# Hedgehog attention gated by a SwiGLU block: the last stage's transposes move from TensorE to VectorE, and its small products take two token tiles in one run

## The chip, the core and the metric

The kernel runs on one core of a Trainium2 chip. The metric is the device time of one execution in microseconds. The core has a matmul engine (TensorE, "PE" in the profile, with its weight loads listed apart as "PEld"), VectorE ("DVE"), ScalarE ("ACT"), GpSimd ("POOL") and a queue that starts transfers (SyncE, "SP"). Each engine works its own instructions in order and waits for others on semaphores.

## The reference

With x of 2048 tokens by 1024 channels, everything in float32:

```python
xn = layernorm(x)
q, k, v = split(xn @ wqkv)                      # 32 heads of 32 channels
pq, pk = per head: q @ w_phi, k @ w_phi
phi_q = concat(softmax(pq), softmax(-pq))       # 64 features per head
phi_k = concat(softmax(pk), softmax(-pk))
kv = phi_k^T v ;  z = sum over tokens of phi_k
o  = (phi_q kv) / (phi_q z + 1e-6)              # per head
s  = o @ wo
g  = silu((silu(xn @ w1) * (xn @ w3)) @ w2)
out = x + s * g
```

## The kernel before

Tokens come in 16 tiles of 128. Large float32 products are made of three passes of a high and a low part (`split` makes them: ScalarE casts the high part, VectorE subtracts it), and by Strassen's scheme with seven products for eight. The stages, in order of time:

1. Layer norm, the operands, and `xn @ w1`, `xn @ w3` (up to about 1160 us).
2. Passes one and two: keys and values, `kv` and `z`.
3. Pass three (`queries`, about 1493 to 1646 us): eight pairs of tiles. `spikes` turns 16 heads of one tile (128x512) into exponentials `e` (128x1024: for each head 32 exponentials of p - max and 32 of min - p) and stores them to DRAM (`e_d`). It is called four times for a pair. A list `later` holds VectorE's less urgent work; one item of it is issued per product. The two tiles of `EARLY` are weighted here already (their sums, factors and scaling run through `later`).
4. The product with `w2`: seven blocks `kb` of eight steps, one pair of tiles each, to about 2170 us. In the last block ScalarE forms the gate (`gate`), which goes to DRAM (`g_d`), and the buffers that come free take what the last stage needs.
5. The last stage (from about 2170 us), whose order is written out by hand for all engines, one tile per turn of the loop:
   - `load_e` brings `e` of a tile back. `weigh` (GpSimd) multiplies it with z; `add_up` (VectorE) sums `e` and the weighted `ez` over each 32 values; `factors` makes the factors out of the sums; `scale` multiplies `e` by them (one half on VectorE, one on GpSimd).
   - `turned`: 16 TensorE transposes of 128x128, and four ScalarE copies out of PSUM (`et`).
   - `heads_out`: 32 small products (64 rows by 32 columns, 128 tokens) with `kvu` into `po`, and `split` of `po` into the operands `oT`.
   - `half_out`: 24 matmuls of 128x512 with `wos` into `pm`, twice a tile, once for each half of the output columns.
   - `result`: VectorE multiplies `pm` by the gate, GpSimd adds x, a transfer stores the half row.

TensorE's order in a turn is: 16 transposes of the next tile, 24 matmuls, 32 small products of the next tile, 24 matmuls. A float32 product that isn't split takes two records of the trace, so the 32 small products show as 64.

Of the kernel before, what the change touches and what calls it, by code (L numbers as in the profile page):

```python
# [21 lines left out]
G = 8  # L22
# [6 lines left out]
def tile_kernel(ctx: ExitStack, tc: tile.TileContext, x, wkT, wqT, wv, wphi, wo, w1, w3, w2, out):  # L29
# [49 lines left out]
    e_d = [[dram.tile([P, D], F, name=f"e_d{i}_{c}") for c in range(2)] for i in range(NT)]  # L79
# [3 lines left out]
    kvu_d = dram.tile([P, 2 * G, DH], F, name="kvu_d")  # L83
# [632 lines left out]
    early, later = {}, []  # L716

    def spikes(t, c, p, e, scaling=False):

        mm = small.tile([P, 2, 16], F, name="mm2")  # L720
        p3 = p.rearrange("p (h f) -> p h f", f=DH)
        nc.vector.tensor_reduce(mm[:, 0, :], p3, axis=AX.X, op=OP.max)
        nc.vector.tensor_reduce(mm[:, 1, :], p3, axis=AX.X, op=OP.min)
        e4 = e.rearrange("p (h s f) -> p h s f", s=2, f=DH)
        nc.vector.tensor_sub(e4[:, :, 0], p3, mm[:, 0, :].unsqueeze(2).to_broadcast([P, 16, DH]))
        nc.vector.tensor_sub(e4[:, :, 1], mm[:, 1, :].unsqueeze(2).to_broadcast([P, 16, DH]), p3)
        nc.scalar.activation(e, e, AF.Exp)
        if not scaling:
            nc.scalar.dma_start(e_d[t][c], e)
            return  # L730

        ef = e.rearrange("p (h f) -> p h f", f=DH)
# [3 lines left out]
        sm, by, rho = early["s"][0][:, c], early["s"][1][:, c], small.tile([P, 2, 16], F, name="rho")  # L736
# [17 lines left out]
        def scale():  # L754
            nc.vector.tensor_mul(ef, ef, by.rearrange("p h s -> p (h s)").unsqueeze(2).to_broadcast([P, H, DH]))
            nc.sync.dma_start(e_d[t][c], e)

        later.extend((sum_e, sum_ez, factors, scale))

    EARLY = (3, 5)  # L760
# [5 lines left out]
    def queries(i, xo, wb, steps, pend):  # L766

        t0, t1 = pairs[i]
        if i == EARLY[0] - 1:
            early["z"] = [flat(bpa.tile([P, 2, 512], R, name="ze", tag=f"ra{6 + c}").bitcast(F)) for c in range(2)]  # L770
            load_z(early["z"])
        for an, pb in seven(xo, wb):
# [3 lines left out]
            elif an == "A12":  # L776
# [4 lines left out]
                spikes(t0, 0, k0, early["e"][0] if i in EARLY else e01[:, 0], i in EARLY)  # L781
# [3 lines left out]
            elif an == "S1":  # L785
                if pend:
                    kv(*pend)
                    kv_out(1, pkv)
                d1 = work.tile([P, 512], F, name="d1", tag="w")
                nc.scalar.copy(d1, pb)  # L790
            elif an == "S3":
                nc.vector.tensor_add(d1, pb, d1)
                spikes(t1, 1, d1, e01[:, 1])
            elif an == "S4":
                nc.vector.tensor_add(d0, pb, d0)
                e10 = rwp.tile([P, 2, 1024], F, name="eq", tag="rw")
                spikes(t0, 1, d0, early["e"][1] if i in EARLY else e10[:, 0], i in EARLY)
            else:
                spikes(t1, 0, pb, e10[:, 1])
# [88 lines left out]
    for c in range(3):  # L888
# [5 lines left out]
        for i in range(len(pairs)):  # L894
# [33 lines left out]
            assert not (end and later)  # L928
            xo = nxt
        wb = wbn  # L930
    close("big")
# [6 lines left out]
    def acc_of(i):  # L938
        for j, t in enumerate(pairs[i]):
            if t not in acc:  # L940
                tag = f"acc{t}" if i < 4 else "acc" + "EEEZZZWW"[2 * i - 8 + j]
                acc[t] = accp.tile([P, 2, 512], F, name=f"acc{t}", tag=tag, bufs={"E": 3, "Z": 3, "W": 2}.get(tag[3], 1))
# [4 lines left out]
    wos, es, ez, sums, by = {}, {}, {}, {}, {}  # L947
# [10 lines left out]

    TILES = [pairs[i][0] for i in EARLY]
    TILES += [t for t in range(NT) if t not in TILES]  # L960
    E_TAGS = (("0", "4"), ("2", "6"), ("1", "5"), ("7", "W"))

    def load_e(i):

        es[i] = []
        for c in range(2):
            tag = E_TAGS[i % 4][c]
            es[i].append(accp.tile([P, 1024], F, name="e", tag=f"acc{tag}", bufs=2 if tag == "W" else 1))
            nc.sync.dma_start(es[i][c], e_d[TILES[i]][c])

    def weigh(i, c):

        t = accp.tile([P, 1024], F, name="ez", tag="accE", bufs=3)
        nc.gpsimd.tensor_mul(t, es[i][c], zb[c])  # L974
        ez[i, c] = t

    def add_up(i, c):

        if c == 0:
            sums[i] = small.tile([P, 2, 2, 16, 2], F, name="sums")  # L980
        for m, src in enumerate((es[i][c], ez.pop((i, c)))):
            nc.vector.tensor_reduce(sums[i][:, m, c].rearrange("p h s -> p (h s)"), src.rearrange("p (h f) -> p h f", f=DH),
                                    axis=AX.X, op=OP.add)

    def factors(i, eng, rho, den):

        sm = sums.pop(i)
        by[i] = small.tile([P, 2, 16, 2], F, name="by")
        nc.vector.reciprocal(rho, sm[:, 0, :, :, 1])
        eng.tensor_mul(rho, sm[:, 0, :, :, 0], rho)  # L990
        eng.tensor_mul(den, sm[:, 1, :, :, 1], rho)
        eng.tensor_add(den, sm[:, 1, :, :, 0], den)
        nc.vector.reciprocal(by[i][:, :, :, 0], den)
        eng.tensor_mul(by[i][:, :, :, 1], by[i][:, :, :, 0], rho)

    def scale(i, c, eng, f=None):

        f = by[i][:, c] if f is None else f
        e3 = es[i][c].rearrange("p (h f) -> p h f", f=DH)
        eng.tensor_mul(e3, e3, f.rearrange("p h s -> p (h s)").unsqueeze(2).to_broadcast([P, H, DH]))  # L1000
# [31 lines left out]
    for r, new in enumerate(steps):  # L1032
# [10 lines left out]
        for b, an, bn in TURN:  # L1043
# [3 lines left out]
            elif old:  # L1047
                product(*old, banks, r, second, b, an, bn)
                if new is None and bn == "T1":
                    load_wo(14)  # L1050
                    load_wo(15)
        if new:
            second = a_second(*parts) if r else ready[1]
        if 8 <= r < 24:
            c, j, s = (r - 8) // 8, (r - 8) // 2 % 4, r % 2
            q = 64 * (j % 2) + 32 * s
            nc.sync.dma_start(kvu_d[q:q + 32, G * c + j // 2:G * c + G:2], kv_d[c][32 * j:32 * j + 32, 4 * s:4 * s + 4])
# [4 lines left out]
        if i + 1 == len(pairs):  # L1062
            if end:
                for k in range(8, 14):
# [6 lines left out]
        if end:  # L1071
            if i:
                gate(*pairs[i - 1])
            if i in (1, 2):
                for k in range(4 * i - 4, 4 * i):
                    load_wo(k)
# [3 lines left out]
            elif i == 2:  # L1080
                load_e(0)
            elif i == 4:
                load_e(1)
                load_e(2)
            elif i == 5:
                kvu = accp.tile([P, 2 * G, DH], F, name="kvu", tag="acc3")
                nc.sync.dma_start(kvu, kvu_d)
        old, banks = new, bank
    close("ps")
# [4 lines left out]
    gate(*pairs[-1])  # L1094
    in_order(ENG.PE, ENG.SP, ENG.Activation, ENG.DVE, ENG.Pool)
    load_e(3)
    weigh(2, 0)
    weigh(2, 1)
    stat = ps.tile([P, 2, 256], F, name="stat", bufs=1)
    po = ps.tile([P, 2, 2, 2, P], F, name="po", bufs=1)  # L1100

    def turned(e):

        ets = []
        for m in range(4):
            pt = ps.tile([P, 4, P], F, name="pt2", tag="tr", bufs=3)
            for g in range(4):
                nc.tensor.transpose(pt[:, g, :], e[m // 2][:, (4 * (m % 2) + g) * P:(4 * (m % 2) + g + 1) * P], ident)
            ets.append(work.tile([P, 4, P], F, name="et", tag="w"))
            nc.scalar.copy(ets[m], pt)  # L1110
        return ets

    def heads_out(ets):

        oT = []
        for c in range(2):
            for q in range(2):
                for g in range(4):
                    for hh in range(2):
                        sl = slice(64 * hh, 64 * hh + 64)  # L1120
                        nc.tensor.matmul(po[32 * g:32 * g + 32, hh, c, q], kvu[sl, G * c + 4 * q + g], ets[2 * c + q][sl, g],
                                         start=True, stop=True, skip_group_check=True)
        for c in range(2):
            oT.append(quad("oT"))
            o4 = oT[c].rearrange("p u (h q) t -> p u h q t", q=2)
            split(o4[:, 0], o4[:, 1], po[:, :, c])
        return oT

    def half_out(oT, c):

        p = ps.tile([P, 512], F, name="pm", tag="mm", bufs=2)
        n = 0
        for k in range(8):
            for a, b in PASSES:
                nc.tensor.matmul(p, oT[k // 4][:, a, k % 4], wos[c, k][:, b], start=n == 0, stop=n == 23)  # L1135
# [3 lines left out]
    def load_gx(i, c):  # L1139

        gx[i, c] = accp.tile([P, 2, 512], F, name="gx", tag="accZ", bufs=3)
        t = TILES[i]
        nc.sync.dma_start(gx[i, c][:, 0], g_d[t][:, c * 512:c * 512 + 512])
        nc.sync.dma_start(gx[i, c][:, 1], x[t * P:(t + 1) * P, c * 512:c * 512 + 512])

    def result(i, c, p):

        t = gx.pop((i, c))
        nc.vector.tensor_mul(t[:, 0], p, t[:, 0])
        (nc.vector if i + 1 == NT else nc.gpsimd).tensor_add(t[:, 0], t[:, 0], t[:, 1])  # L1150
        r0 = TILES[i] * P
        nc.sync.dma_start(out[r0:r0 + P, c * 512:c * 512 + 512], t[:, 0])

    gx = {}
    load_gx(0, 0)
    load_gx(0, 1)
    oT = heads_out(turned(es.pop(0)))
    p1 = None
    for i in range(NT):
        nxt = i + 1 < NT  # L1160
        st = stat[:, i % 2]
        rho, den, by0 = (st[:, a:a + 32].rearrange("p (c h) -> p c h", c=2) for a in (0, 32, 64))
# [68 lines left out]
```

## Time and profile before

| | |
|---|---|
| median of three runs | 2406.64 us (2405.56 to 2408.09) |
| profiled execution | 2406.6 us, its span 2404.8 us |
| TensorE busy, share of the span | 2367.7 us, 98% |
| VectorE, ScalarE, GpSimd busy | 73%, 37%, 30% |
| last stage, from the end of the product with w2 | about 2170 to 2404.8 us |
| 768 large matmuls of the last stage | 183.0 us busy |
| 256 transposes, 1024 records of small products | 34.2 us and 18.7 us busy |

Busy times are sums over the instructions of one group; a group's row gives also the mean duration of one. Matmuls overlap their neighbours, so the time from the start of one run of matmuls to the start of the next is read for what a run costs, not the sum of durations. The profiled execution took 1.8 us more than its span.

### The profile page before, as it was taken

What the parts mean: (1) busy time and instruction counts of PE and PEld (TensorE: products, weight loads), DVE (VectorE), ACT (ScalarE), POOL (GpSimd) and SP (SyncE); (2) the same over time, 40 slices, a digit from 0 to 9 for tenths busy, and PEclk for the clock granted to TensorE, in tenths of its full rate; (3) what the DMA queues carried; (4) which work ended last, traced back from release to release, by engine and by line L of the source; (5) the groups of instructions that cost most, each with busy time, mean ns of one, the idle gap of its engine ahead of it and who ended that gap; (6) DMA issues with size and microseconds to landing.
All of it is one profiled execution on the core that took longest, in us unless ns stands there. A gap on an engine that the chain in (4) does not pass through costs nothing.

```text
span 2404.8 us, 36324 instructions
## 1 busy us (share of the span) xinstructions
PE 2367.7 (98%) x13554; PEld 1950.3 (81%) x13554; DVE 1746.5 (73%) x2493; ACT 891.8 (37%) x1566; POOL 726.4 (30%) x511
## 2 busy tenths in 40 slices
PE   5999999999999999999999999999999999999999
PEld 5888888888888888888888788887888888887887
DVE  8567798775688888884676556786677887776664
ACT  6445544443345445443221112334322322243221
POOL 2233555452355555551000000010011111124663
PEclk9999999999999999999999999999999999999999
DMA  7567789877877787877999868987544354466553
GB/s 262 177 213 238 231 293 311 286 248 230 255 274 267 248 284 263 278 250 258 361 329 357 303 190 322 363 330 252 165 156 130 143 182 175 171 242 236 188 177 114
DMA packets 305679, 586.33 MB, mean 244 GB/s; under 512 B 25440, under 2 KB 140384, under 8 KB 302816
## 3 DMA queue, kind: packets, MB, share of 16 engines
q1 hardware_dynamic: 301472, 569.34, 68.4%
q10 hardware_dynamic: 4032, 14.68, 1.5%
q8 instruction: 107, 1.75, 0.3%
q14 instruction: 68, 0.56, 0.1%
HBM read 379.19 MB, written 205.00 MB: 243 GB/s over the span
## 4 chain that ended last, share of the span: by engine, by line
PE 90%; issue 4%; POOL 3%; DVE 1%; DMA 1%; ACT 1%; SPq 0%; POOLq 0%; ACTq 0%; DVEq 0%
PE bankb L622 25%; PE bankb L1013 13%; PE bankc L622 13%; PE bankb L673 11%; PE bankc L1013 6%; PE banka L622 6%; PE bankc L673 5%; PE banka L1013 3%; PE banka L673 3%; PE pm L1135 2%; POOL ez L974 1%; POOL e L1000 1%; PE pkv L659 1%; POOL gx L1150 1%; PE pw L246 1%
## 5 line engine op out<-in xcount | busy, mean ns | idle before, releaser
L92 DVE TENSOR_TENSOR bo<-rw,bo 128x512 fp32r<-128x512 f32 x336 | 310.1, 923 | 147.4 <-ACT bo L91 145.0
L1023 POOL TENSOR_TENSOR acc<-acc,u 128x512 f32<-128x512 f32 x48 | 63.7, 1327 | 476.6 <-ACT u L1022 447.0
L91 ACT CAST bo<-rw 128x512 fp32r<-128x512 f32 x336 | 201.3, 618 | 7.9 <-DMA w_d0T<-w2o 3.2
L1013 PE MATMUL bankb<-bo,as 128*128 128x512 f32 x816 | 200.8, 389 | 0.0
L1135 PE MATMUL pm<-wos,oT 128*128 128x512 f32 x768 | 183.0, 394 | 0.0
L1013 PEld LDWEIGHTS bankb<-bo,as 128*128 128x128 f32 x816 | 153.1, 188 | 32.2 <-ACT acc L1019 0.4
L1135 PEld LDWEIGHTS pm<-wos,oT 128*128 128x128 f32 x768 | 141.9, 188 | 31.8 <-issue 2.8
L622 PE MATMUL bankc<-op0S,bo 128*128 128x512 f32 x672 | 163.1, 391 | 1.4 <-ACT op0S L91 1.4
L622 PE MATMUL bankb<-op0A,bo 128*128 128x512 f32 x672 | 163.3, 391 | 0.3 <-DVE bo L92 0.3
L622 PE MATMUL bankb<-op0S,bo 128*128 128x512 f32 x672 | 162.9, 391 | 0.0
L622 PE MATMUL bankc<-op1S,bo 128*128 128x512 f32 x672 | 161.5, 389 | 0.4 <-issue 0.4
L622 PE MATMUL bankb<-op1S,bo 128*128 128x512 f32 x672 | 161.5, 389 | 0.0
L622 PE MATMUL bankb<-op1A,bo 128*128 128x512 f32 x672 | 161.4, 389 | 0.0
L622 PEld LDWEIGHTS bankc<-op0S,bo 128*128 128x128 f32 x672 | 125.4, 188 | 27.7 <-ACT op0S L91 1.6
L622 PEld LDWEIGHTS bankc<-op1S,bo 128*128 128x128 f32 x672 | 126.0, 188 | 26.9 <-issue 0.7
L1013 PE MATMUL bankc<-bo,as 128*128 128x512 f32 x576 | 146.5, 389 | 1.1 <-ACT as L91 0.7
L622 PEld LDWEIGHTS bankb<-op1S,bo 128*128 128x128 f32 x672 | 126.0, 188 | 26.5 <-ACT wk L564 0.4
L622 PEld LDWEIGHTS bankb<-op1A,bo 128*128 128x128 f32 x672 | 126.1, 188 | 26.2
L622 PEld LDWEIGHTS bankb<-op0A,bo 128*128 128x128 f32 x672 | 125.4, 188 | 26.3 <-DVE bo L92 0.6
L622 PEld LDWEIGHTS bankb<-op0S,bo 128*128 128x128 f32 x672 | 125.4, 188 | 26.2 <-ACT wk L564 0.2
L127 POOL TENSOR_TENSOR rw<-rw 128x512 f32<-128x512 f32 x56 | 86.3, 1541 | 155.0 <-DMA rw<-in_w 137.1
L1013 PEld LDWEIGHTS bankc<-bo,as 128*128 128x128 f32 x576 | 108.0, 188 | 24.3 <-ACT as L91 1.1
(246 smaller groups left out, 4730.2 us busy)
## 6 DMA issues: line engine op xcount, KB each, us to landing
rw<-in_w SPq DMA_DIRECT2D x224, 256.0 KB, 3.5
hr<-h_d SPq DMA_DIRECT2D x56, 512.0 KB, 3.7
xoS<-xo_d0S SPq DMA_DIRECT2D x48, 512.0 KB, 9.3
xoS<-xo_d1S SPq DMA_DIRECT2D x48, 512.0 KB, 6.2
xoA<-xo_d0A SPq DMA_DIRECT2D x36, 512.0 KB, 7.8
xoA<-xo_d1A SPq DMA_DIRECT2D x36, 512.0 KB, 6.9
e<-e_d SPq DMA_DIRECT2D x32, 512.0 KB, 3.7
h_d<-wk SPq DMA_DIRECT2D x56, 256.0 KB, 3.6
```

What stands on the lines that cost most here:

```text
L91: nc.scalar.copy(hi, src)
L92: (by or nc.vector).tensor_sub(lo, src, hi.bitcast(F))
L127: nc.gpsimd.tensor_sub(b12, b22, b12)
L246: nc.tensor.matmul(pw[:, g, :], wr[:, g], bd[:, 4 * c + g, :], start=True, stop=True)
L622: nc.tensor.matmul(bank, bt[:, w, kk], aos[tb][an][:, u, kk], start=an in ("A11", "A12", "S1") and n == 0, stop=LAST[b] == an and n == 11, ...
L659: nc.tensor.matmul(pkv[sl, m], e[:, m // 4, (m % 4) * P + 32 * h:(m % 4) * P + 32 * h + 32], v[:, 4 * (m % 4) + h], start=first and m == 0 ...
L673: nc.tensor.matmul(bank[b], xo[an][:, u, k], wb[bn][:, w, k], start=an in ("A11", "A12", "S1") and n == 0, stop=LAST[b] == an and n == 11, ...
L974: nc.gpsimd.tensor_mul(t, es[i][c], zb[c])
L1000: eng.tensor_mul(e3, e3, f.rearrange("p h s -> p (h s)").unsqueeze(2).to_broadcast([P, H, DH]))
L1013: nc.tensor.matmul(bank[b], t[:, u, pos + k], bos[kb, bn, k][:, w], start=first and n == 0, stop=LAST[b] == an and n == 5, skip_group_chec ...
L1023: nc.gpsimd.tensor_add(c, c, u)
L1135: nc.tensor.matmul(p, oT[k // 4][:, a, k % 4], wos[c, k][:, b], start=n == 0, stop=n == 23)
```

## The change

- **Transposes.** `turned` goes. VectorE transposes squares of 32x32 instead (`swap`): four instructions for each half `c` of the heads, two tiles, each 128x512. Two tiles of tokens are interleaved: `e_d` holds two tiles in 256 rows, and `load_e` reads each second row, so that a block of 64 neighbouring tokens lies beside each other after the squares of both tiles are written with a stride of two.
- **Small products.** After the squares, a group of 32 partitions holds 32 features of a head for 64 tokens. So `heads_out` makes, for two tiles at once, 256 products of 32 rows by 32 columns with 64 tokens, and adds the two halves of the features (`s`) in PSUM. `po` is four banks. `kvt` is the small matrix, loaded four times, once for each group of partitions.
- **Loop.** One turn is now two tiles (8 turns): TensorE runs 24, 24 matmuls, the 256 small products of the next two tiles, 24, 24 matmuls. `split` of `po` becomes `operands` with four halves.
- **Sums.** The sums of `e` are made in pass three (`later`, one 128x1024 reduction for each `spikes`), kept in `s_all`, stored to `s_d` and read back as `s_in`. One of the two subtractions of `spikes` goes to GpSimd (three calls of four), and the early tiles' scaling as well. `ez` is made and summed in pieces of 512.
- **Around it.** Which buffers the accumulators, `e`, `et` and the gate take is set anew; the first squares (`swap(0, ..)`) and the first weighting (`weigh(1, 0)`) are made in the last block of the product with w2.

Core of the diff:

```diff
-    def turned(e):
-        ets = []
-        for m in range(4):
-            pt = ps.tile([P, 4, P], F, name="pt2", tag="tr", bufs=3)
-            for g in range(4):
-                nc.tensor.transpose(pt[:, g, :], e[m // 2][:, ...], ident)
-            ets.append(work.tile([P, 4, P], F, name="et", tag="w"))
-            nc.scalar.copy(ets[m], pt)
+    def swap(b, c):
+        for q in range(2):
+            ets[c, q] = accp.tile([P, 16, 32, 2], F, name="et", tag=f"acc{4 + 2 * c + q}")
+            for t in range(2):
+                nc.vector.transpose(ets[c, q][:, :, :, t], es[b, t, c][:, 512 * q:512 * q + 512])
...
-                        nc.tensor.matmul(po[32 * g:32 * g + 32, hh, c, q], kvu[sl, G * c + 4 * q + g], ets[2 * c + q][sl, g],
-                                         start=True, stop=True, skip_group_check=True)
+            for k in range(4):
+                hh, q = k // 2, k % 2
+                for s in range(2):
+                    for a in range(4):
+                        sl = slice(32 * a, 32 * a + 32)
+                        for g in range(4):
+                            at_ = 2 * (2 * g + hh) + s
+                            k0, n0 = 64 * (4 * c + k), 32 * (16 * q + at_)
+                            nc.tensor.matmul(po[32 * g:32 * g + 32, a, k0:k0 + 64], kvt[c][sl, n0:n0 + 32],
+                                             ets[c, q][sl, at_].rearrange("p r t -> p (r t)"),
+                                             start=c == 0 and k == 0 and s == 0, stop=c == 1 and k == 3 and s == 1, ...)
...
     def spikes(t, c, p, e, scaling=False, on=None):
...
-        nc.vector.tensor_sub(e4[:, :, 1], mm[:, 1, :].unsqueeze(2).to_broadcast([P, 16, DH]), p3)
+        (on or nc.vector).tensor_sub(e4[:, :, 1], mm[:, 1, :].unsqueeze(2).to_broadcast([P, 16, DH]), p3)
...
+            later.append(lambda: nc.vector.tensor_reduce(s_all[b // 4][:, b % 4, a, c], ef, axis=AX.X, op=OP.add))
...
+    heads_out()
+    oT = operands()
+    for b in range(NB):
+        p0 = half_out(oT, 0, 0)
+        if b == 0:
+            add_up(1, 1); factors(1); weights(1)
+            swap(1, 0); load_e(3, 0); swap(1, 1); load_e(3, 1); weigh(2, 0)
+        else:
+            result(4 * b - 1, last)
+            swap(b + 1, 1); load_e(b + 3, 1)
+            weigh(b + 2, 1); add_up(b + 2, 1); factors(b + 2)
+        p1 = half_out(oT, 0, 1)
+        result(4 * b, p0)
+        heads_out()
+        p2 = half_out(oT, 1, 0)
+        result(4 * b + 1, p1)
...
+            weights(b + 2); nxt = operands()
+        swap(b + 2, 0); load_e(b + 4, 0)
+        weigh(b + 3, 0)
+        last = half_out(oT, 1, 1)
+        result(4 * b + 2, p2)
+        add_up(b + 3, 0)
```

TensorE at the start of the last stage, before: `pt` are the transposes, `po` the small products, `pm` the large ones; a row counts the program's matmuls.

```order
L1013 MATMUL bankb<-bo,as 128x512 x6
L1108 MATMUL pt_18366<-ident,e 128x128 x4
L1108 MATMUL pt_18373<-ident,e 128x128 x4
L1108 MATMUL pt_18380<-ident,e 128x128 x4
L1108 MATMUL pt_18387<-ident,e 128x128 x4
L1121 MATMUL po<-et,kvu 32x128 x32
L1108 MATMUL pt_18432<-ident,e 128x128 x4
L1108 MATMUL pt_18439<-ident,e 128x128 x4
L1108 MATMUL pt_18446<-ident,e 128x128 x4
L1108 MATMUL pt_18453<-ident,e 128x128 x4
L1135 MATMUL pm<-wos,oT 128x512 x24
L1121 MATMUL po<-et,kvu 32x128 x32
```

The same place in the changed kernel; `late` holds some of the matrices of `wos`.

```order
L1044 MATMUL bankb<-bo,as 128x512 x6
L1157 MATMUL po<-et,kvt 32x64 x256
L1179 MATMUL pm<-wos,oT 128x512 x39
L1179 MATMUL pm<-late,oT 128x512 x9
L1157 MATMUL po<-et,kvt 32x64 x256
L1179 MATMUL pm<-wos,oT 128x512 x39
L1179 MATMUL pm<-late,oT 128x512 x9
```

The transposes are gone; small products now stand between 96 large matmuls each, and the first ones come right behind the product with w2.

VectorE in one turn of the loop before (one tile).

```order
L92 TENSOR_TENSOR oT<-po,oT 128x512 x2
L1149 TENSOR_TENSOR gx<-pm,gx 128x512
L1185 COPY stat<-by 128x32
L1000 TENSOR_TENSOR e<-e,stat 128x1024
L1149 TENSOR_TENSOR gx<-pm,gx 128x512
L982 TENSOR_REDUCE sums<-e 128x32
L982 TENSOR_REDUCE sums<-ez 128x32
L982 TENSOR_REDUCE sums<-e 128x32
L982 TENSOR_REDUCE sums<-ez 128x32
L989 RECIPROCAL stat<-sums 128x32
```

VectorE in one turn now (two tiles), from the factors' last copy on.

```order
L1017 COPY stat<-by 128x64
L1198 TENSOR_TENSOR gx<-pm,gx 128x512 x2
L1024 TENSOR_TENSOR e<-e,stat 128x1024 x2
L93 TENSOR_TENSOR oT<-po,oT 128x512 x4
L1031 STREAM_TRANSPOSE et<-e 128x512 x4
L1198 TENSOR_TENSOR gx<-pm,gx 128x512
L1003 TENSOR_REDUCE zs<-ez 128x16 x4
L1198 TENSOR_TENSOR gx<-pm,gx 128x512
L1031 STREAM_TRANSPOSE et<-e 128x512 x4
L1003 TENSOR_REDUCE zs<-ez 128x16 x4
L1011 RECIPROCAL stat<-s_in 128x64
```

Eight transposes (`STREAM_TRANSPOSE`) stand where the four reductions of `e` stood, and the factors are made once for two tiles.

VectorE in the first turn now, where the order differs: everything for the second two tiles stands in one row of work behind the first `operands`.

```order
L93 TENSOR_TENSOR oT<-po,oT 128x512 x4
L1003 TENSOR_REDUCE zs<-ez 128x16 x4
L1011 RECIPROCAL stat<-s_in 128x64
L1012 TENSOR_TENSOR stat<-s_in,stat 128x64
L1013 TENSOR_TENSOR stat<-zs,stat 128x64
L1014 TENSOR_TENSOR stat<-zs,stat 128x64
L1015 RECIPROCAL by<-stat 128x64
L1016 TENSOR_TENSOR by<-by,stat 128x64
L1017 COPY stat<-by 128x64
L1024 TENSOR_TENSOR e<-e,stat 128x1024 x2
L1031 STREAM_TRANSPOSE et<-e 128x512 x8
L1198 TENSOR_TENSOR gx<-pm,gx 128x512 x2
```

The second run of small products on TensorE waits for the eight transposes at the end of this row.

More of the change, by code (lines that the diff above doesn't have):

```diff
@@ L768, in queries @@
         t0, t1 = pairs[i]
+        if i == 0:
+            s_all.extend(work.tile([P, 4, 2, 2, 32], F, name="s_all", tag="h1", bufs=2) for _ in range(2))
+            nc.gpsimd.memset(s_all[0][:, 0], 1.0)
         if i == EARLY[0] - 1:
@@ L927, in tile_kernel @@
             pend = (queries if c == 2 else heads)(i, xo, wb, steps(), pend)
-            assert not (end and later)
             xo = nxt
         wb = wbn
+    while later:
+        later.pop(0)()
+    for h in range(2):
+        for a in range(2):
+            nc.sync.dma_start(s_d[h][P * a:P * a + P], s_all[h][:, :, a])
     close("big")
@@ L985, in factors, with load_e @@
[L985 to L1000, printed above, removed]
+    def load_e(b, c):
+        if b < NT // 2:
+            for t in range(2):
+                es[b, t, c] = accp.tile([P, 1024], F, name="e", tag=f"acc{(0, 8)[b % 2] + 2 * c + t}")
+                nc.sync.dma_start(es[b, t, c], e_d[b][c][t::2])
@@ L1191, in tile_kernel @@
+    result(4 * NB - 1, last)
     in_order()
```

287 lines of the change are left out of this document (167 added, 120 removed).

## The prediction

> **What bounds the kernel now.** I read the page first: which engine fills the span.
>
> ```profile
> span 2404.8 us, 36324 instructions
> PE 2367.7 (98%) x13554; PEld 1950.3 (81%) x13554; DVE 1746.5 (73%) x2493; ACT 891.8 (37%) x1566; POOL 726.4 (30%) x511
> ```
>
> TensorE works 98% of the span, so time is won only where it issues less, or sooner. Next, busy time by stretch, for two stretches of pass three and one of the last stage (columns: window, length, then busy us of PE, PEld, DVE, ACT, POOL, the clock, the DMA share, GB/s).
>
> ```profile
> 1510.00:1530.00 20.00, 20.00 (x90) 16.57 (x89) 11.82 (x19) 6.59 (x8) 0.00 (x0) 1.00 0.99 372
> 1550.00:1570.00 20.00, 20.00 (x90) 16.57 (x89) 19.74 (x36) 5.50 (x8) 4.62 (x2) 1.00 0.90 329
> 2220.00:2240.00 20.00, 19.95 (x170) 16.00 (x176) 14.65 (x25) 4.14 (x8) 14.10 (x8) 1.00 0.64 209
> ```
>
> TensorE is full in all three, at full clock. In pass three VectorE has 8 us of 20 free with an ordinary pair, none with an early one, and even then TensorE doesn't wait. In the last stage no other engine is full. So the last stage is TensorE's own work, and the timeline of TensorE prices it (start, length, what; a length runs to the modelled end of the last matmul, so costs are taken from start to start).
>
> ```profile
> 2197.98 5.75 PE L1135 MATMUL pm<-wos,oT 128*128 128x512 f32 x24
> 2203.58 2.23 PE L1108 MATMUL pt<-ident,e 128*128 128x128 f32 x16
> 2205.57 5.72 PE L1135 MATMUL pm<-wos,oT 128*128 128x512 f32 x24
> 2211.22 1.16 PE L1121 MATMUL po<-et,kvu 64*32 64x128 f32 x64
> 2212.30 5.76 PE L1135 MATMUL pm<-wos,oT 128*128 128x512 f32 x24
> 2225.48 1.16 PE L1121 MATMUL po<-et,kvu 64*32 64x128 f32 x64
> ```
>
> A tile takes 2225.48 - 2211.22 = 14.26 us: 24 large matmuls 5.60 or 5.65, the transposes 1.99, the small products 1.08. Two tiles: 28.52.
>
> **The small products now: the price that decides.** 256 products are 512 records (32 showed as 64). No row has a 32x32 form. The nearest two, each with the duration of one record:
>
> ```profile
> 1407.10 0.77 PE L659 MATMUL pkv<-ev 128*32 128x34 f32 x64
> L659 PE MATMUL pkv<-ev x2048: 191/197/218, 1164.5 to 1491.1; 128*32 128x34 f32 x187
> L1121 PE MATMUL po<-et,kvu x1024: 269/269/294, 2172.7 to 2383.4; 64*32 64x128 f32 x171
> ```
>
> A run's length less one duration, over 63 gaps: (1.16 - 0.27)/63 = 14.1 ns for `po`, (0.77 - 0.20)/63 = 9.1 ns for `pkv`. `po` has eight places in the array (64x32), so one place takes 8 x 14.1 = 113 ns for 128 columns. If streaming alone set the pace, `pkv` with 34 columns and four places would take 113 x 34/128/4 = 7.5 ns; it takes 9.1, so there the issue of load and matmul seems to limit. The new form (64 columns, 16 places) would stream in 113/2/16 = 3.5 ns. Bounds: 3.5 and 14.1 ns. I take 9.1, the row with the shortest products, which also go to a new place after each pair of records. A run ends with 1.08 - 64 x 0.0141 = 0.18 us of changeover. So one run costs 512 x 0.0091 + 0.18 = 4.84 us (between 2.0 and 7.4).
>
> The Trainium skill, "TensorE: Matmul & The Clock Gate", Part 1, says that start-to-start never falls below about 25 ns however few columns; an estimate by that page is 512 x 25 ns = 12.8 us a run, some 65 us more over eight runs, about 2463 us. The trace disagrees in its two tiled forms (14.1 and 9.1 ns). The same page, Part 3, adds about 4 ns for each tile of a packed group, an estimate of 2.0 us a run; no row here shows that pace.
>
> **The sum, part by part.**
>
> *Transposes and small products.* Before 16 x (1.99 + 1.08) = 49.1 us. Now 8 x 4.84 = 38.7. Term: -10.4.
>
> *Fewer breaks between large matmuls.* The end of the chain shows 72 in a row:
>
> ```profile
> 2383.63 16.57 PE pm L1135 x72
> ```
>
> ```profile
> L1135 PE MATMUL pm<-wos,oT 128*128 128x512 f32 x768 | 183.0, 394 | 0.0
> ```
>
> With the 0.39 us of one record (the group's row) taken off, (16.57 - 0.39)/71 = 0.228 us each; 24 take 5.47 instead of 5.60 in the timeline. 32 x 0.13: -4.2.
>
> *The start of the stage.* Timeline of TensorE, VectorE and ScalarE:
>
> ```profile
> 2155.98 1.52 PE L1013 MATMUL bankb<-bo,af 128*128 128x512 f32 x6
> 2169.59 1.47 PE L1108 MATMUL pt<-ident,e 128*128 128x128 f32 x12
> 2169.79 0.69 DVE L1025 TENSOR_TENSOR acc<-bankb,acc 128x512 f32<-128x512 f32 x1 [0.68 <-PE bankb L1013]
> 2174.12 0.59 ACT L91 CAST oT<-po 128x512 fp32r<-128x512 f32 x1 [0.61 <-PE po L1121]
> 2174.73 0.69 DVE L92 TENSOR_TENSOR oT<-po,oT 128x512 fp32r<-128x512 f32 x1 [4.25 <-ACT oT L91]
> 2177.00 5.26 PE L1135 MATMUL pm<-wos,oT 128*128 128x512 f32 x22
> ```
>
> Before, 7.41 us pass from 2169.59 to 2177.00, of which 2 x 1.99 + 1.08 are work: 2.35 idle. Now the small products may wait for VectorE's last eviction (until 2170.48, since `po` takes four banks), 0.9, and the large ones for cast and subtraction of the first operand, 0.59 + 0.69. Term: -0.2. The first transposes lie in the last block, where TensorE sets the pace: nothing.
>
> *VectorE and GpSimd in a turn.* Groups of the last stage (busy, mean ns), and VectorE's timeline:
>
> ```profile
> L974 POOL TENSOR_TENSOR ez<-e,zb 128x1024 f32<-128x1024 f32 x28 | 67.5, 2428 | 28.4 <-DMA e<-e_d 18.0 <-ACT acc L956 7.0 <-DMA g_d<-acc 3.4
> L1150 POOL TENSOR_TENSOR gx<-gx 128x512 f32<-128x512 f32 x30 | 38.6, 1287 | 87.9 <-DVE gx L1149 72.9 <-DVE stat L1185 9.9 <-issue 5.1
> L1000 POOL TENSOR_TENSOR e<-e,by 128x1024 f32<-128x1024 f32 x14 | 26.9, 1918 | 0.0
> L993 DVE RECIPROCAL by<-stat 128x32 f32<-128x32 f32 x14 | 5.0, 358 | 0.5
> 2227.31 0.69 DVE L92 TENSOR_TENSOR oT<-po,oT 128x512 fp32r<-128x512 f32 x1 [2.38 <-ACT oT L91]
> 2228.65 0.69 DVE L92 TENSOR_TENSOR oT<-po,oT 128x512 fp32r<-128x512 f32 x1 [0.65 <-ACT oT L91]
> 2229.26 0.68 DVE L1149 TENSOR_TENSOR gx<-pm,gx 128x512 f32<-128x512 f32 x1
> 2229.86 0.18 DVE L1185 COPY stat<-by 128x32 f32<-128x32 f32 x1
> 2235.28 1.21 DVE L982 TENSOR_REDUCE sums<-e 128x32 f32<-128x1024 f32 x1
> 2236.40 1.21 DVE L982 TENSOR_REDUCE sums<-ez 128x32 f32<-128x1024 f32 x1
> 2237.53 0.35 DVE L989 RECIPROCAL stat<-sums 128x32 f32<-128x32 f32 x1
> 2238.99 0.19 DVE L994 TENSOR_TENSOR by<-by,stat 128x32 f32<-128x32 f32 x1
> ```
>
> From start to start VectorE needs 0.60 us for 128x512 and 1.13 for 1024; cast and subtraction alternate, 1.34 an operand. The factors took 2237.53 to 2239.2, 1.65 us, for 32 columns; for 64, two reciprocals and five short operations, with the copy, I estimate 2.5. A transpose of 128x512 is in no row: at least 0.60 (same elements in and out), at most 1.13 (if it moved half as much a cycle, the price of twice the elements). I take 0.60, that of the same shape. A turn: transposes 8 x 0.60, sums of `ez` 8 x 0.60, scalings 2 x 1.13, operands 4 x 1.34, results 4 x 0.60, factors 2.5: 22 us. GpSimd: 4 x 2.43 + 2 x 1.92 + 4 x 1.29 = 18.7. TensorE's turn is 4 x 5.47 + 4.84 = 26.7. The longest loop over both engines is: factors 2.5, two results 1.2, scalings 2.3, operands 5.4, transposes 2.4, a result, four sums and a result 3.6, GpSimd's addition 1.3, four pieces of `ez` 4.9, the last sum 0.7: 24.3. It fits with 2.4 to spare. ScalarE only loses work.
>
> *The first two turns aren't steady.* Count from the end of the first small products. VectorE: operands 5.4, four sums 2.4, factors 2.5, scalings 2.3, four transposes 2.4: 15.0; four more, behind GpSimd's scalings (10.3 + 3.8 = 14.1): 17.4. TensorE wants the second run of small products at 1.3 + 10.5 = 11.8, waits until 15.0, and works its second half behind the later transposes: +3.2. In the second turn VectorE's order is operands, eight sums (the later four need `ez` buffers that the first four free), factors, scalings, transposes, and only then the result that frees the third bank of `pm`: 19.8 + 5.4 + 5.2 + 2.5 + 2.3 + 2.4 + 0.6 = 38.2, while TensorE wants the bank at 19.8 + 3 x 5.47 = 36.2: +2.0. Term: +5.2.
>
> *Pass three.* An ordinary pair gets four sums and loses three subtractions on VectorE: 4 x 1.13 - 3 x 0.60 = +2.7 us onto some 12 of 19: hidden under TensorE. Early pairs get lighter (two scalings, three subtractions off; two sums on). GpSimd, idle there, works the subtractions in about 1.3 each (the 128x512 addition above). What is queued behind: ScalarE's exponential waits for the slower of two engines, and its copies out of PSUM stand behind it; SyncE's four stores of the sums wait for the last sum, with the next loads of `bo` behind them. At the turn to the next stage TensorE waits already:
>
> ```profile
> 1649.19 0.73 PE L1013 MATMUL bankc<-bo,as 128*128 128x512 f32 x2 [0.66 <-ACT as L91]
> 1650.37 1.20 PE L1013 MATMUL bankc<-bo,as 128*128 128x512 f32 x4 [0.44 <-DVE as L92]
> ```
>
> That is 1.1 us; I add as much again: +1.0, between 0 and +3.
>
> *Transfers.* `e` moves the same bytes in rows of 4 KB; `kvt` (eight loads) may start once the last step's first six matmuls have read their operand, at 2157.5 by the row of 2155.98, 12 us ahead; SyncE has the loads of the first gate behind the last gate's store, but the first results come late enough. Nothing.
>
> Sum: -10.4 - 4.2 - 0.2 + 5.2 + 1.0 = -8.6. The profiled execution, 2406.6 us, stands at the median (2406.64): 2398.
>
> **The rivals.**
>
> A. Small products stream: 2.0 us a run, 22.7 us less, but then the 24.3 us loop sets the turn instead of 23.9 (about +2): 2378. For it: no row has more than eight places, so 9.1 isn't shown to be a floor. Against: no row is faster. Chance 0.12.
>
> B. Slower than before: small products stay at 14.1 ns, since 16 places with four banks written at once overlap no better than eight. 7.4 us a run, +20.5: 2418. It decides from 8.6/8 = 1.1 us more a run, 5.9 us or 11.2 ns, on. For it: that is the pace of `po` itself; against: `po`'s columns are twice as many. Chance 0.15, of which 0.03 for a still higher floor.
>
> C. Transposes at 1.13: eight stand in the first turn's path (+4.2), four in the second's (+2.1), and the loop grows to 26.4, level with TensorE: 2404. For it: 4-byte elements written with a stride; against: every 128x512 row costs 0.60. Chance 0.16.
>
> D. Pass three stalls TensorE by a us a pair, because a sum or a copy stands behind exponentials that wait for GpSimd: +8, about 2406, no change. Against: the early pairs ran VectorE full without a stall. Chance 0.08.
>
> **How the numbers follow.** My forecast has 0.49 (2393 to 2403 as its own range). 0.2% is 4.8 us, about what a measurement of this kernel can tell from no change. Faster: most of the forecast, A and a third of C: 0.62. Same: D, two thirds of C, some of B: 0.20. Slower: the rest of B: 0.18. The range leaves out half of A and the upper part of B: 2383 to 2412.
>
> **What would show it.** In the profile after: runs of `po` of 512 records from start to next start near 4.84 us; large matmuls at 5.47 per 24 between them; transposes of 0.6 to 0.7 us; TensorE waiting some 3 us for VectorE's transposes before the second run and 2 us for a result in the second turn, and nowhere later; pass three's length unchanged to 1 us. A pace above 11 ns, or a turn above 28.5 us, makes the prediction wrong.

## The result, and the profile after

The changed kernel takes 2505.53 us (median of 4 runs, 2503.27 to 2509.79) against 2406.86 us: 1.0412 times as long, 95% interval 1.0394 to 1.0430. The forecast was 2398. The profiled execution took 2504.26 us. Its page first (of part 2 only the granted clock, in 40 slices of 62.6 us; of part 3 only the larger of the two instruction queues):

```profile
span 2502.1 us, 41951 instructions
...
PE 2390.2 (96%) x16370; PEld 1970.4 (79%) x16370; DVE 1759.2 (70%) x2507; ACT 856.7 (34%) x1502; POOL 762.9 (30%) x569
...
PEclk9999999999999999999999999999999999968878
...
q8 instruction: 129, 2.11, 0.3%
```

TensorE has fallen from 98% to 96%, no other engine's share has risen, and in these slices the granted clock drops in the last stage alone. The instruction queue brought 107 packets before and 129 now, of 2.11 MB / 129 = 16.4 KB each. TensorE executed 2 x 13554 matmuls and weight loads before and 2 x 16370 now; at 256 a packet that makes 105.9 and 127.9 packets, so this queue brings TensorE's instructions.

Between the two traces 97 us of span lie as follows. The last stage, from TensorE's first instruction in it to its last: 230.6 us before, 310.3 now, +79.7. The loops between pass three and it: +11.7. Pass three: 142.3 to 145.1, +2.8. Ahead of pass three, where TensorE's instructions are the same: +3.2. Pass three starts at 1492.16 us before and at 1495.32 now; in the nine experiments below it starts between 1492.3 and 1494.9, so I take that as scatter.

The last stage by groups (busy, mean ns of one | idle before, what ended it; `po` are the small products, `pm` the large ones):

```profile
L1179 PE MATMUL pm<-wos,oT 128*128 128x512 f32 x624 | 161.2, 420 | 1.7 <-issue 1.0 <-ACT oT L92 0.7
...
L1157 PE MATMUL po<-et,kvt 32*32 32x64 f32 x4096 | 55.9, 272 | 61.9 <-issue 60.5 <-DVE acc L1056 0.8 <-DVE et L1031 0.6
...
L1031 DVE STREAM_TRANSPOSE et<-e 128x512 f32<-128x512 f32 x56 | 34.6, 678 | 0.0
L1179 PE MATMUL pm<-late,oT 128*128 128x512 f32 x144 | 35.2, 389 | 0.0
```

Ahead of the small products TensorE stood 60.5 us "issue": it waited for nothing that the profile shows. The large matmuls were busy 161.2 + 35.2 = 196.4 us instead of 183.0. Transposes and small products together took 52.9 us before, small products alone 55.9 now. So 61.5 of issue, 13.4 of slower large matmuls and 3.0 make up 78 of the 79.7.

Where in a run the 60.5 us lie, TensorE's timeline shows: the first run, then the first piece of three later ones, one of them whole with the large matmuls behind it.

```profile
2187.20 1.98 PE L1157 MATMUL po<-et,kvt 32*32 32x64 f32 x179 [0.78 <-DVE acc L1056]
2193.56 1.95 PE L1157 MATMUL po<-et,kvt 32*32 32x64 f32 x128 [4.38 <-issue]
2199.50 1.96 PE L1157 MATMUL po<-et,kvt 32*32 32x64 f32 x128 [3.98 <-issue]
2205.43 1.36 PE L1157 MATMUL po<-et,kvt 32*32 32x64 f32 x77 [3.98 <-issue]
2207.48 10.83 PE L1179 MATMUL pm<-wos,oT 128*128 128x512 f32 x39 [0.68 <-ACT oT L92]
...
2299.93 2.11 PE L1157 MATMUL po<-et,kvt 32*32 32x64 f32 x194
2303.84 1.96 PE L1157 MATMUL po<-et,kvt 32*32 32x64 f32 x128 [1.79 <-issue]
2308.95 1.96 PE L1157 MATMUL po<-et,kvt 32*32 32x64 f32 x128 [3.16 <-issue]
2312.42 1.08 PE L1157 MATMUL po<-et,kvt 32*32 32x64 f32 x62 [1.51 <-issue]
2313.43 10.75 PE L1179 MATMUL pm<-wos,oT 128*128 128x512 f32 x39
...
2326.07 9.00 PE L1179 MATMUL pm<-wos,oT 128*128 128x512 f32 x39
...
2337.04 2.41 PE L1157 MATMUL po<-et,kvt 32*32 32x64 f32 x225
...
2374.09 2.71 PE L1157 MATMUL po<-et,kvt 32*32 32x64 f32 x257
```

The run of 512 records, forecast at 4.84 us, takes 20.28 the first time (2187.20 to 2207.48) and 13.50 here (2299.93 to 2313.43). It comes in pieces: a first one of 160 to 259 records, then pieces of exactly 128, and a rest. A record is a matmul with its weight load, so 128 records are 256 instructions; one packet of 16.4 KB for each piece makes 64 bytes an instruction. The first piece grows by 32 from turn to turn (194, 225, 257): a turn has 512 + 96 = 608 records, which is five times 128 less 32, so the breaks stand at fixed places of the program, one every 128 records. Inside a piece the pace is (1.96 - 0.27)/127 = 13.3 ns at a low clock and, at full clock, (1.48 - 0.27)/127 = 9.5 ns (a piece of the spread products below).

The trace lists each packet with its start, and that ties the gaps to the queue. In the run of 2299.93, packets of the instruction queue start at 2301.56, 2306.61 and 2310.03 us, and the next pieces start at 2303.84, 2308.95 and 2312.42, each 2.3 to 2.4 us later. All 23 gaps of over 0.5 us in the stage end so, 2.2 to 3.1 us after the start of such a packet.

Two windows, over the first run and over one of the later ones (columns as in the prediction, the last three being the granted clock, the DMA share and GB/s):

```profile
2187.00:2207.00 20.00, 7.25 (x512) 6.20 (x512) 0.14 (x1) 0.16 (x1) 0.00 (x0) 0.59 0.91 366
2300.00:2314.00 14.00, 7.54 (x514) 6.46 (x514) 2.95 (x3) 0.46 (x1) 11.14 (x8) 0.62 0.35 117
```

TensorE is busy a third to a half of the time, the granted clock falls to 0.6, and the 39 large matmuls behind a run take 10.75 us (clock 0.86 from 2314 to 2324 us), the next 39 again 9.00 (1.00 from 2326 to 2335). The gaps differ between the two (4 us, and 1.5 to 3.2), and so does the DMA share (0.91 and 0.35). That mean hides a busy and a quiet stretch, the second and third pieces of the run:

```profile
2304.00:2309.00 5.00, 1.84 (x135) 1.55 (x133) 0.00 (x0) 0.00 (x0) 5.00 (x5) 0.50 0.75 254
2309.00:2312.40 3.40, 1.92 (x128) 1.62 (x128) 0.00 (x0) 0.00 (x0) 2.19 (x2) 0.50 0.02 7
```

From start to start the two pieces take 5.11 and 3.47 us: even with the DMA engines all but idle a block takes longer than the 1.96 us that its records need. Share and spacing don't go together everywhere (from 2271.55 to 2275.29, 3.74 us at a share of 0.76).

The second place is the turn from pass three to the next loop: SyncE's queue, and TensorE.

```profile
1625.29 24.37 SPq L954 DMA_DIRECT2D s_d<-s_all  x4
1649.76 1.07 SPq L856 DMA_DIRECT2D bo<-w_d0T  x2
```

```profile
1655.07 2.90 PE L1044 MATMUL bankb<-bo,as 128*128 128x512 f32 x6 [6.76 <-DMA bo<-w_d0T]
```

The four stores of the sums hold SyncE for 24.4 us, since the last sum starts at 1647.9; the loads of weights behind them start at 1649.76 and TensorE waits 6.76 us for them, then takes 2.69 us instead of 1.36 for six matmuls (clock 0.50 from 1655 to 1658 us).

### The profile page after: what moved, and what is told of

Read it like the earlier page. It is cut to its first block, busy times and chain, and to the rows that moved or that the text cites. A ratio compares the mean times of both kernels' runs of the same rounds, so it can differ in the third digit from the quotient of the medians.

```text
span 2502.1 us, 41951 instructions
## 1 busy us (share of the span) xinstructions
PE 2390.2 (96%) x16370; PEld 1970.4 (79%) x16370; DVE 1759.2 (70%) x2507; ACT 856.7 (34%) x1502; POOL 762.9 (30%) x569
## 3 DMA queue, kind: packets, MB, share of 16 engines
q8 instruction: 129, 2.11, 0.3%
## 4 chain that ended last, share of the span: by engine, by line
PE 90%; issue 3%; DMA 3%; DVE 3%; ACT 1%; SPq 1%; POOL 0%; ACTq 0%; POOLq 0%; DVEq 0%
PE bankb L623 23%; PE bankb L1044 12%; PE bankc L623 12%; PE bankb L674 9%; PE pm L1179 7%; PE bankc L1044 6%; PE banka L623 6%; PE bankc L674 5%; PE banka L1044 3%; PE banka L674 2%; PE po L1157 2%; PE pkv L660 1%; PE pw L247 1%; SPq L165 0%; PE pt L218 0%
## 5 line engine op out<-in xcount | busy, mean ns | idle before, releaser
L1179 PE MATMUL pm<-wos,oT 128*128 128x512 f32 x624 | 161.2, 420 | 1.7 <-issue 1.0
L1179 PEld LDWEIGHTS pm<-wos,oT 128*128 128x128 f32 x624 | 127.5, 206 | 32.1 <-issue 3.4
```

Source lines behind the costliest of these rows:

```text
L1179: nc.tensor.matmul(p, oT[a, k // 4][:, u, k % 4], wos[c, k][:, w], start=n == 0, stop=n == 23)
```

## The experiments

**Supply or array?** My theory by now: TensorE runs out of instructions, which come in blocks of 256. The rival: small products in 16 places simply take that long.

```
-   nc.tensor.matmul(po[32 * g:32 * g + 32, a, k0:k0 + 64], kvt[c][sl, n0:n0 + 32],
-                    ets[c, q][sl, at_].rearrange("p r t -> p (r t)"),
+   k1, a1 = min(k0, 384), min(at_, 14)
+   nc.tensor.matmul(po[32 * g:32 * g + 32, a, k1:k1 + 128], kvt[c][sl, n0:n0 + 32],
+                    ets[c, q][sl, a1:a1 + 2].rearrange("p h r t -> p (h r t)"),
...
```

> Each small product takes 128 columns of the exponentials instead of 64, with as many instructions in the same order; it computes other values, so only its time is read. Theory (supply): in the changed kernel TensorE's run of 512 records breaks into a first piece and pieces of exactly 128 records with 1.5 to 4.8 us between them, because its instructions come too slowly; twice the columns then change the pace in a piece by at most a few ns and the gaps shrink by what the pieces grow: 2500 to 2515 us, the same pieces of 128. Rival (array): the products themselves take about 14 us a run, by their columns or the places they share; then a run doubles, +8 x 14 = about 110 us, some 2615 us, and the pieces aren't of 128.

It took 2507.82 us (one run; the kernel before 2407.21). The later pieces of the first run on TensorE's timeline:

```profile
2193.31 2.58 PE L1158 MATMUL po<-et,kvt 32*32 32x128 f32 x128 [3.75 <-issue]
2199.25 2.81 PE L1158 MATMUL po<-et,kvt 32*32 32x128 f32 x128 [3.36 <-issue]
2205.18 2.01 PE L1158 MATMUL po<-et,kvt 32*32 32x128 f32 x77 [3.13 <-issue]
```

The pieces are 0.6 to 0.9 us longer, yet they start 5.94 and 5.93 us apart, as in the changed kernel (2193.56, 2199.50, 2205.43). What sets their starts is not what they do. Over the stage "issue" falls from 60.5 to 49.0 us while the time stays. The rival falls.

**Half of the products, and a quarter.**

```
-                for s in range(2):
+                for s in range(1):
...
```

> Leaves out half of the features of the small products: 256 records a run instead of 512; it computes other values, so only its time is read. Theory (supply): the first 160 to 257 records of a run come without a break, so a run has one gap at most instead of three: about 2.4 us of work and 0 to 4 us of gap instead of some 14 us, 8 x 9 to 11 us less: 2415 to 2435 us, and the granted clock stays above 0.9 after the first run. Rival (array): a run costs in proportion to its records, half of 14 us: 8 x 7 = 56 us less, about 2450 us, and the clock still falls.

2432.29 us, as the supply would have it. What TensorE waited for, and two of the later runs:

```profile
PE po L1157 <- issue: 16.7, 6, 5.0
PE pm L1179 <- issue: 4.6, 2, 2.4
```

```profile
2239.24 1.80 PE L1157 MATMUL po<-et,kvt 32*32 32x64 f32 x162
2245.07 1.50 PE L1157 MATMUL po<-et,kvt 32*32 32x64 f32 x94 [4.03 <-issue]
...
2327.93 2.97 PE L1157 MATMUL po<-et,kvt 32*32 32x64 f32 x256
2330.83 0.50 PE L1179 MATMUL pm<-wos,oT 128*128 128x512 f32 x1
2333.73 11.55 PE L1179 MATMUL pm<-wos,oT 128*128 128x512 f32 x38 [2.40 <-issue]
```

One gap a run instead of three. In the second of these runs all 256 records pass without a break, and the gap comes one record later, at a large matmul: it belongs to the place in the program, not to the small products. I was wrong that the clock would stay up: one gap is enough (11.55 us for 38, at a granted clock of 0.75).

Then 128 records a run, to see a run within what lies ready (columns 128, so that every column is written):

```
-            for k in range(4):
+            for k in (0, 2):
...
-                for s in range(2):
+                for s in range(1):
...
```

> Leaves out three quarters of the small products (a run of 128 records of 128 columns); it computes other values, so only its time is read. Theory (supply): 160 to 257 records lie ready when a run starts, so 128 come without a gap, each run takes some 2 us, the granted clock stays at 1.00 in the large matmuls behind it (9.0 us for 39 instead of 10.2 to 11.6): from the kernel with half the products 21 us of gaps, 16 us of slow matmuls and 10 us of products go, and up to 6 come back where VectorE's and GpSimd's loop of 24.3 us is longer than the turn: 2385 to 2393 us. Rival (a run has a gap whatever its length, as a price of the change of form): a gap of 2 to 5 us and a low clock remain in each run, 2405 to 2415 us.

2394.66 us (one run; the kernel before beside it 2405.8), 2 us above my range. TensorE's waits in the last stage, and two turns:

```profile
PE pm L1179 <- DVE gx L1198: 3.4, 1, 3.4
PE po L1157 <- DVE et L1031: 1.9, 2, 1.3
```

```profile
2257.81 1.90 PE L1157 MATMUL po<-et,kvt 32*32 32x128 f32 x128
2259.64 9.13 PE L1179 MATMUL pm<-wos,oT 128*128 128x512 f32 x39
...
2281.62 1.90 PE L1157 MATMUL po<-et,kvt 32*32 32x128 f32 x128
```

No gap of issue is left in the stage, and the large matmuls keep their pace behind a run that nothing interrupts (9.13 us for 39). Behind the one run that waited for transposes (0.63 and 1.30 us) they took 11.50. So 128 small products by themselves don't lower the clock. I put the 2 us down to VectorE: the waits for transposes and for a result in the first two turns, which the supply's gaps had covered in the changed kernel.

**The same products, spread.**

```
-        for c in range(2):
-            for k in range(4):
+        for part in parts:
+            c = part // 2
+            for k in (2 * (part % 2), 2 * (part % 2) + 1):
...
+                if n in between:
+                    heads_out((between[n],))
...
+        apart = 0 < b < NB - 1
+        p0 = half_out(oT, 0, 0, {12: 0} if apart else {})
+        p1 = half_out(oT, 0, 1, {4: 1, 20: 2} if apart else {})
+        p2 = half_out(oT, 1, 0, {12: 3} if apart else {})
```

> The same small products as in the changed kernel, but in six of the eight runs they stand in four parts of 128 records among the 96 large matmuls of a turn (after 12, 28, 44 and 60) instead of in one run of 512; the first two runs stay whole. Theory (supply): behind each part stand matmuls that need 0.23 us for one pair of instructions, so the supply catches up: no gaps in the six turns, a turn of about 27 us instead of 36 to 38, so 6 x 8 to 10 us less: about 2450 us (2440 to 2465). Rival (array): the products cost the same wherever they stand, 2505 us or somewhat more, since each part brings a changeover.

2456.16 us (2453.34 to 2461.58), 1.0202 times the kernel before (1.0182 to 1.0222): 49.4 less than the changed kernel, with the same instructions. Timeline of one turn, its first rows and the next turn's first:

```profile
2250.22 1.75 PE L1158 MATMUL po<-et,kvt 32*32 32x64 f32 x128
2251.90 3.92 PE L1182 MATMUL pm<-wos,oT 128*128 128x512 f32 x16
...
2278.78 1.48 PE L1158 MATMUL po<-et,kvt 32*32 32x64 f32 x128
```

The turn takes 2278.78 - 2250.22 = 28.56 us without a gap, where the same work took 37.05 in the changed kernel (2337.04 to 2374.09). "Issue" falls from 60.5 to 27.7 us, most of it in the first two runs, which stayed whole. But 28.56 is also what two tiles took before (28.52): the parts take 4 x 1.41 (2278.78 to 2280.19, where the next large matmul starts), and 96 large matmuls with four breaks the other 22.9 us instead of the 21.9 forecast.

**Does data traffic slow the supply?**

```
+        if 0 < b < NB - 1:
+            for k in range(8):
+                nc.sync.dma_start(copies[k], e_d[k // 2 % 4][k % 2][b % 2::2])
```

> The changed kernel with eight copies of 512 KB more in each of six turns, from memory to memory, ahead of the run of small products; what it computes stays. Theory (the supply shares the DMA engines with the data): pieces then follow each other at the 5.9 us of the first run, made while the engines were full, instead of 3.5 to 5.1: three gaps a run by some 1.5 us more, 6 x 4.5 = about +27 us, 2530 us. Rival (the supply has its own pace whatever the traffic): pieces as before, 2505 us; a wait of the large matmuls for late loads would show as such.

2532.09 us (one run). The turn that the changed kernel has at 2299.93, and a window over it:

```profile
2297.48 2.12 PE L1159 MATMUL po<-et,kvt 32*32 32x64 f32 x194
2304.45 1.97 PE L1159 MATMUL po<-et,kvt 32*32 32x64 f32 x128 [4.85 <-issue]
2310.94 1.96 PE L1159 MATMUL po<-et,kvt 32*32 32x64 f32 x128 [4.52 <-issue]
2316.87 1.08 PE L1159 MATMUL po<-et,kvt 32*32 32x64 f32 x62 [3.97 <-issue]
```

```profile
2300.00:2314.00 14.00, 3.93 (x256) 3.35 (x256) 0.54 (x1) 0.00 (x0) 8.71 (x7) 0.53 1.00 340
```

With the DMA engines full (share 1.00 instead of 0.35) the gaps are 4.85, 4.52 and 3.97 us instead of 1.79, 3.16 and 1.51, and "issue" over the stage is 86.6 us instead of 60.5: 26.1 more, about as much as the whole time grew (26.6). Data traffic does slow the supply. The page's part 3 counts the instruction packets on the same 16 DMA engines as the data; whether these engines or the memory behind them make the packets late isn't shown.

**The turn to the next loop.** The four stores of the sums are moved to the third step of that loop, behind its first loads:

```
-    for h in range(2):
-        for a in range(2):
-            nc.sync.dma_start(s_d[h][P * a:P * a + P], s_all[h][:, :, a])
...
+        if r == 2:
+            for h in range(2):
+                for a in range(2):
+                    nc.sync.dma_start(s_d[h][P * a:P * a + P], s_all[h][:, :, a])
```

> Only the four stores of the exponentials' sums move on SyncE: from the end of pass three to the third step of the next loop, behind the first loads of its weights. Theory (queue): TensorE waits 6.8 us at the turn for weights whose loads stand behind these stores; that wait and the lower clock behind it go: 8 to 10 us less, about 2496 us. Rival (transfers): the weights come late since the DMA engines are full or since VectorE is late there; then no change, 2505 us.

2494.61 us (2490.74 to 2495.01), 1.0356 times the kernel before (1.0341 to 1.0372): 10.9 less. The row of the 6.8 us is gone from the waits, of which at the turn 0.6, 0.7 and 0.4 us are left. The loops between pass three and the last stage take 536.7 us, 546.8 in the changed kernel and 535.1 before.

Both edits together:

> Both edits together: the small products of six runs in four parts among the large matmuls, and the four stores of the sums moved behind the next loop's first loads. Theory (two separate causes, supply in the last stage and SyncE's queue at the turn): their gains add, 2505.5 - 49.4 - 10.9 = 2445 us (2440 to 2450). Rival (one cause behind both, such as the granted clock after a stall): less than the sum, 2452 us or more.

2445.75 us (2444.21 to 2447.25), 1.0154 times the kernel before (1.0137 to 1.0171): the gains add to within a microsecond. These are two causes.

**Finer parts** (eight of 64 records, and the second run spread as well):

```
-        p0 = half_out(oT, 0, 0, {12: 0} if apart else {})
+        p0 = half_out(oT, 0, 0, {4: 0, 13: 1, 22: 2} if apart else {})
...
-        p1 = half_out(oT, 0, 1, {4: 1, 20: 2} if apart else {})
+        p1 = half_out(oT, 0, 1, {7: 3, 16: 4} if apart else {})
...
-        if b == 0:
-            heads_out()
-        p2 = half_out(oT, 1, 0, {12: 3} if apart else {})
+        p2 = half_out(oT, 1, 0, {1: 5, 10: 6, 19: 7} if apart else
+                      {k: n for n, k in enumerate((0, 3, 6, 9, 12, 15, 18, 21))} if b == 0 else {})
```

> As the kernel with both edits, but the products stand in eight parts of 64 records, 9 large matmuls apart in six turns, and the second run is spread too, in eight parts 3 matmuls apart; only the first run stays whole. Theory (supply, one block of 128 pairs per 3.5 to 6 us): most of the 11 us of gaps of the second run and of the 6 us left in the six turns go: 2430 us (2424 to 2438). Rival (changes between small and large products): each change costs some 0.1 to 0.2 us, 8 x 6 more parts' ends eat the gain: 2445 us or more. Either way no faster than the kernel before, since even the turns without a gap took 28.56 us with four parts, against 28.52 for two tiles before.

2452.91 us (2451.91 to 2456.15): slower than with four parts, in the rival's range, but not only at the rival's price. TensorE's waits from the loop ahead on:

```profile
PE po L1159 <- issue: 17.4, 7, 4.4
PE po L1159 <- DVE et L1028: 8.7, 1, 8.7
```

Issue went from 24.8 to 17.4 us, but I had put the first part of the second turn ahead of the transposes it needs: 8.7 us of waiting. And a turn without a gap took 29.76 us (2274.56 to 2304.32) instead of 28.56: 0.3 us for each break more. So both a misplaced part and the breaks ate the gain.

**Pass three.** Subtractions back on VectorE (with the stores moved):

```
-        (on or nc.vector).tensor_sub(e4[:, :, 1], ...)
+        nc.vector.tensor_sub(e4[:, :, 1], ...)
```

> The stores moved as before, and the subtractions of pass three back on VectorE (they are on GpSimd in the changed kernel); compare with the kernel that has the stores moved alone, 2494.6 us. Theory: pass three is 2.8 us longer since exponentials wait for GpSimd (5.9 us longest) and ScalarE's copies stand behind them: TensorE's waits of 0.9 to 1.3 us for these copies go: 2491 to 2493 us. Rival: VectorE, with four sums more per pair, is the late one; then its load grows by 3 x 0.6 us a pair and pass three gets longer: 2495 to 2500 us.

2500.43 us (2492.36 to 2501.02), against 2494.61 (2490.74 to 2495.01): no gain, rather a loss of 0.2%, about as much as the runs scatter. TensorE's waits from pass three on to the next loop, with the stores moved alone and then with the subtractions back:

```profile
PE bankc L674 <- ACT d L810: 1.2, 2, 0.9
PE bankb L674 <- ACT k L794: 0.9, 1, 0.9
```

```profile
PE bankb L674 <- ACT k L794: 2.6, 1, 2.6
PE bankb L674 <- DVE d L812: 2.4, 1, 2.4
```

A new wait for VectorE (2.4) appears and the one for ScalarE's copy grows: the rival holds. Pass three takes 148.9 us, 144.7 with the stores moved alone, so the subtractions cost less on GpSimd than on VectorE. In the eight profiles that share its code with the changed kernel's it took 144.1 to 145.6 us, 142.3 before; what in it costs these 2 to 3 us isn't settled.

## Why the prediction was wrong, point by point

*A run of small products, 512 x 0.0091 + 0.18 = 4.84 us.* This is the step that failed. The pace was right (9.5 ns in a piece at full clock), and rival B's 14.1 wrong. But I took it from runs of 64 records and carried it to 512 as though instructions were always there; the eight runs took 11.7 to 20.3 us. Both rows that gave a pace lie within what TensorE holds ready; the longest piece without a gap of issue was 259 records. Counted by blocks of 128 records, a tile before is exactly one (24 + 24 large, 16 transposes, 64 products) in 14.26 us; a turn now is 608/128 = 4.75 in a forecast 26.7, of which four in 4.84 us. The instruction queue's row shows it, over the last stage before and after:

```profile
q8 instruction: 16, 0.26, 0.5%
```

```profile
q8 instruction: 38, 0.62, 0.8%
```

In the long runs a block comes every 3.5 to 6.8 us. At 5.9 us, 38 blocks alone need 224 us, nearly the whole 230.6 of the stage before, so at that rate even an even spread leaves hardly a gain. Nothing in my prediction counted them. The Trainium skill, "Runtime: NRT & Kernel Launch", section "Instruction fetch mechanics", has blocks of 256 instructions and two of them held at a time, with which the pieces agree to within a few records (at most 259, that is 518 instructions). The 2048 instructions that it also gives for TensorE they don't bear out, and its statement there that crossing into the next block is mostly hidden doesn't hold for this run.

*Fewer breaks, -4.2.* Where nothing was lacking this came true (in the trace of the quarter, 48 matmuls in 11.0 us, 5.5 per 24); in the changed kernel the low clock behind each gap turned it into +13.4. The granted clock wasn't in the sum at all.

*The estimate by a floor.* 2463, worked out from the 25 ns of the Trainium skill, "TensorE: Matmul & The Clock Gate", Part 1, stood nearer the result than my sum, but by luck. The trace doesn't show that floor: in a piece a record takes 9.5 ns. The mean over a run, 23 to 40 ns (11.7 to 20.3 us for 512), is made of gaps.

*Transposes, 0.60 start to start.* Right: 34.6/56 = 0.62 us of VectorE's time each. Rival C falls. *The first two turns, 3.2 + 2.0 us.* In the changed kernel the gaps covered them (0.6 and 0); in the kernel with a quarter of the products they stood uncovered at 1.9 and 3.4. That their sum is right is partly luck, since the runs there take 1.9 us instead of 4.84. The first half was also summed wrong: 48 large matmuls at 5.47 per 24 are 10.9 us, not 10.5, which makes 2.8 of the 3.2. *VectorE's loop of 24.3 us* was too long by at least 0.5, since there a turn of 23.81 us ran without waiting for it.

*Pass three, +1.0.* Its inner part came to +2.8, within the bounds, with stalls in few places (rival D's shape, not its size). What failed is the turn behind it: I named SyncE's stores with the loads of `bo` behind them and then priced only TensorE's old wait doubled. The queue row would have given more: the stores hold SyncE until the last sum, and the loads start at 1649.76 us, with the stores moved at 1629.10. It measured 10.9 us.

*Transfers, nothing.* TensorE waits for no data transfer in the last stage, but transfers lengthen the gaps: 5.9 us and more a block with the engines full.

The sum: -8.6 forecast; in its place stand about +80 in the last stage, +12 from the turn on, +3 in pass three. The chances don't add up either: "slower" has 0.18 as the rest of B, but B has 0.15 in all, and no rival was a shortage of instructions.

## What to carry to other kernels

Count instructions, not only microseconds: a long run of matmuls that are much shorter than their fetch is paced by the instruction queue, here 128 load-and-matmul pairs per 3.5 to 6.8 us with at most some 260 ready at the start. Either keep such a run to a block's length (128 pairs ran without a gap), put long matmuls between the pieces (37.05 us a turn became 28.56), or leave the work in fewer, larger instructions. And where a store waits for a late result, look at what stands behind it in its queue before you price the store.

## What the runs showed of the hardware that I had not expected

- TensorE's instructions come in blocks of 256, start to start 5.94 and 5.93 us in a loaded stretch whatever the pieces hold (1.95 or 2.8 us of work), and still 3.47 us with the DMA engines at a share of 0.02. A packet of the queue takes 0.9 to 1.8 us, and work goes on 2.2 to 3.1 us after its start.
- The fetch gets slower with data traffic: with 24 MB of copies added over six turns, "issue" rose from 60.5 to 86.6 us.
- One gap of 2.4 us is enough for a lower clock over the next 10 us: 11.55 us for 38 matmuls, at a granted clock of 0.75, instead of 8.8. Two waits of 0.63 and 1.30 us did as much: 11.50 for 39.
- Products of 32x32 with 64 columns pass at 9.5 ns a record, those with 128 columns at (1.90 - 0.29)/127 = 12.7 ns: twice the columns cost a third more, not twice as much.
